# A transformer block on one core: a new written-out order for about nine hundred operations

## The chip, the core and the metric

The kernel runs on one core of a Trainium2 chip. The metric is the device time of one execution in microseconds (us). Five instruction streams run side by side, each in its own order: TensorE (PE in the profile: matrix products; PEld are its weight loads), VectorE (DVE), ScalarE (ACT), GpSimd (POOL), and SyncE (SP), which here only issues DMAs: loads, stores and transposing copies. An instruction that waits for another engine holds up everything behind it in its own stream.

## The reference

The input x has 2048 rows (one batch) of D = 640, bf16. There are H = 32 heads of 20 and F = 1536.

```python
def _A_ref(x, wqkv, w_phi, wo):
    ... # q, k, v = heads of x @ wqkv
    pq = jnp.einsum("bhsd,hdf->bhsf", q, w_phi)
    pk = jnp.einsum("bhsd,hdf->bhsf", k, w_phi)
    phi_q = jnp.concatenate([_softmax(pq, axis=-1), _softmax(-pq, axis=-1)], axis=-1)
    phi_k = jnp.concatenate([_softmax(pk, axis=-1), _softmax(-pk, axis=-1)], axis=-1)
    kv = jnp.einsum("bhsf,bhsd->bhfd", phi_k, v)
    z  = jnp.einsum("bhsf->bhf", phi_k)
    num = jnp.einsum("bhqf,bhfd->bhqd", phi_q, kv)
    den = jnp.einsum("bhqf,bhf->bhq", phi_q, z)[..., None] + 1e-6
    o = num / den
    return (...) @ wo          # heads put side by side again
def _B_ref(x, w_gate, w_up, w_down):
    return ((x @ w_gate) * (x @ w_up)) @ w_down     # written as einsums
x = A_x
h = x + _A_ref(_layernorm(x, axis=-1), A_wqkv, A_w_phi, A_wo)
h2 = h + _B_ref(_layernorm(h, axis=-1), B_w_gate, B_w_up, B_w_down)
return h2
```

The attention is linear: the sum over all rows (`kv`, `z`) must be complete before the first row of `num` can be formed. The block ends with a gated product without a nonlinearity.

## The kernel before

**Tiles.** The rows are cut into 16 tiles of 128. An operation's name carries its tile: Qb5 is operation Qb of tile 5. Line numbers are those of the kernel before; the changed file's are 21 lower from `class Buf` on, since its table of the order has 21 lines fewer.

**Preparation.** `w_phi` is folded into the K and Q parts of `wqkv` on TensorE. Loads of x and weights (L285) are x0, x1, x2, x3, x4, x6, x8, x10, x12, x14 (the later ones two tiles each), wk, wv, w5, wg, wu, wd, wo. Ph0 to Ph2 (L380, POOL or DVE) lay out `w_phi`; WT0 to WT4 (L392) transpose the K weights on TensorE and WTe copies them out; F1_0 to F1_4 (L411) are the five K folds, F0_0 to F0_4 the five Q folds, and Fe copies each out of PSUM. The Q weights are transposed by SP's DMAs wqt0 to wqt4 (L309). Before that, small products warm0 to warm21 (L367, L372) run on zeros.

**Attention, per tile t.** L1s, L1a (L428, L431, DVE), L1l, L1e (L436, L439, ACT) and L1n (L443, one element per row, POOL or DVE) give the statistics of the first normalisation; xn (L453 on DVE, L451 on ACT) applies it; xt transposes the result, on TensorE for tiles 0 and 1 (L462, copied out by xte, L251), by an SP DMA for the others (L471). V, K and Q (L482) are projections of ten matmuls of 320 columns each (for tiles 0 and 1 cut into five pairs, K0_0 to K0_4). Ve copies V out of PSUM (L251, `evac`, ACT or DVE). Of K, Kx (L494, ACT, two instructions) takes exp of plus and minus the value, Ks (L498, DVE) sums over each head, Kr and Ke (L501, L503, ACT) form the reciprocal through ln and exp, Kn (L518, POOL) multiplies, and KV (L526, eleven small matmuls) adds to `kv` and `z`, which stay in two PSUM banks until KVe (L533, DVE) takes them out. Of Q, Qx (L551 and a small L553, ACT, twice) takes the exps, Qs (L556, DVE) sums, Qr (L559, ACT) takes the ln, Qb (L563, POOL or DVE, 32 elements per row) subtracts, Qe (L566, ACT) takes an exp, Qn (L570, POOL) scales one half, and qT (L575) is an SP transposing DMA. N (L588) is the product with `kv`; dd, rl, rd (L602, L606 to L612, DVE or ACT) prepare the division and o (L615, DVE) does it; oT (L619) is an SP transposing DMA; O (L625) the product with `wo`.

**Second part, per tile and block.** h (L631, DVE) adds the residual and sums the row; hc (L639 on DVE, L640 on ACT) centres; hT (L653) is an SP transposing DMA; L2q (L642, ACT), L2v (L646, POOL or DVE, one element per row) and L2r (L649, DVE) give the row's scale, which is applied only at the end. The gate and up products U (L668) run over blocks of tiles: block 0 is tiles 0 and 1, block 1 tiles 2 to 5, block 2 tiles 6 to 9, block 3 tiles 10 to 13, block 4 tiles 14 and 15, each in 12 pieces of F, gate and up apart (U1_3_0 is block 1, piece 3, gate). g (L673, ACT) copies the gate product out, u (L676, DVE) multiplies. D (L687) is the down product of a tile, y (L699, DVE) scales and adds, w (L701) stores. Tile 15's down product is cut into three pieces.

**What sets the order.** Nothing is scheduled on the chip. A table, PLAN, holds for each operation a number, which engine of its alternatives it uses, and which buffers of a pool it takes:

```python
    _f = _t.split(":")
    PLAN[_f[0]] = (float(_f[1]), int(_f[2] or 0) if len(_f) > 2 else 0,
                   tuple(int(_v) for _v in _f[3].split(",")) if len(_f) > 3 else ())
```

`Graph.op` reads the entry; `alts` lists the engine of the code first and the other one second, so `Qb5:369:1` means rank 369, second engine (for Qb: POOL first, DVE second; for Ve: ACT first, DVE second). `arrange` sorts all operations by the number and appends each to its engine's stream:

```python
    for o in sorted(G.ops, key=lambda o: (o.key, o.i)):
        o.start = o.key
        order[o.eng].append(o)
```

It also adds the waits that follow from a buffer taken a second time. `emit` turns all dependences into waits on the engines' counters, leaving out those that another wait already covers. The numbers in the table are used for sorting alone. The table of before holds times in us, that of the changed kernel ranks from 0 to 1029.

Of the kernel before, what the change touches and what calls it, by code (L numbers as in the profile page):

```python
# [53 lines left out]
x1:0.78:1 ekz:0.78 x0:0.78 zero:0.91 id0:1.014 warm0:1.127 id1:1.252 x3:1.26:1 wk3:1.26:1 warm1:1.345 va1:1.496 warm2:1.564 w5:1.74:1 warm3:1.782 warm4:2.001  # L54
warm5:2.219 wk0:2.22:1 eps:2.326 gl0:2.357 warm6:2.437 gla:2.518 warm7:2.656 wk4:2.7:1 glb:2.822 warm8:2.874::0 warm9:3.093 wk1:3.18 warm10:3.311 warm11:3.529
wk2:3.66:1 L1s1:3.725 warm12:3.748 warm13:3.966 x4:4.14 warm14:4.185 warm15:4.403 L1s0:4.512 wv1:4.62 warm16:4.621 warm17:4.84 wv0:5.1:1 L1a1:5.299 L1s3:5.408
WT3:5.446::1 L1l1:5.532 wv2:5.58:1 Ph2:5.775 L1e1:5.858 warm18:5.902 warm19:6.011 wv3:6.06 WTe3:6.1:1 warm20:6.12 L1a0:6.195 xn1:6.304::0 Ph1:6.369 x2:6.54
# [4 lines left out]
wqt1:12.163 L1s2:12.225 L1e4:12.321 V0_0:12.369::6 K1_4:12.64 V1_1:12.911 L1n5:13.012:1 Kx1_0:13.11::0 V0_1:13.182 xn5:13.296::3 V0_2:13.453 Kx1_1:13.694
V0_3:13.724 L1a2:13.826 xt5:13.934 L1s7:13.935 V0_4:13.995 K0_2:14.266 L1l2:14.278 K0_3:14.537 L1e2:14.604 Ve0:14.697::0 Ks1:14.722::0 V1_2:14.808 L1n2:14.884
V1_3:15.079 Sz:15.108 wqt0:15.244 xn2:15.281:1:0 L1n4:15.287 V1_4:15.35 K3:15.621::4 L1s6:16.115 Kr1:16.234 Ke1:16.525 xt2:16.554 x12:16.671:1 Kn1:16.859
K0_4:16.977 L1a6:17.025 xn4:17.134::1 Kx3_0:17.177::1 V3:17.248::6 L1s8:17.664 Kx3_1:17.761 wqt2:17.864 Ve1:18.345::1 L1a7:18.451 L1s9:18.56 K5:18.604::4
L1l6:18.929 xt4:19.174 L1e6:19.255 Ks3:19.347::1 Ve3:19.348::2 L1n7:19.535 L1n6:19.759 Kx0_0:19.932::2 V5:19.96::0 rqz:19.983 wqt3:20.484 Kx0_1:20.516
xn7:20.74::2 Kx5_0:21.1::3 xn6:21.27::3 K2:21.316::6 Kx5_1:21.684 L1a8:21.8 xt6:21.908 L1a9:21.909 Ks0:22.018::2 Kr3:22.268 Ke3:22.559 V2:22.672::2
Ve5:22.705::3 Kn3:22.893 xt7:23.218 Kx2_0:23.289::4 Ks5:23.411::3 Kx2_1:23.873 V4:24.028::4 Ve2:24.457::4 x10:24.528 L1s12:24.804 x14:25.008 L1l8:25.041
L1e8:25.367 F0_0:25.384::0 Kr0:25.46 wg2:25.488 Ks2:25.591::0 L1n8:25.647 F0_2:25.703::6 Ke0:25.751 L1n9:25.871 Ve4:25.897::5 wg0:25.968 V6:26.022::2 Kn0:26.095
Fe0_0:26.481 L1s13:26.984 xn9:27.065:1:0 F0_4:27.378::4 K4:27.697::0 Kr5:27.88 Fe0_4:27.895:1 xt9:28.018 Ve6:28.026::6 mk0:28.408 mk1:28.572 Kr2:28.61  # L70
L1s11:28.635 Ke2:28.901 Fe0_2:29.047 KV0:29.053::4,5 Kn2:29.235 wd1:29.328 KV1:29.386 L1s10:29.422 Kx4_0:29.631::2 K7:29.719::2 L1s14:30.209 Kx4_1:30.215
F0_3:31.075::6 L1a14:31.119 L1a10:31.228 Kx7_0:31.275::0 xn8:31.337::1 V7:31.394::0 smz:31.548 Fe0_3:31.859 L1a11:31.867 xt8:31.975 Ks4:31.976::1 Kx7_1:32.443
KV2:32.75 Ke5:33.027 KV3:33.083 L1l10:33.173 wg1:33.285 L1s15:33.369 F0_1:33.416::6 L1e10:33.499 K6:33.735::2 L1n11:33.779 Fe0_1:33.933 Kn5:34.003
L1n10:34.156:1 L1a13:34.331 xn11:34.44::3 Kr4:34.517 Ve7:34.663::7 L1a15:34.97 xt11:35.078 L1a12:35.079 K9:35.091::6 Ks7:35.188::2 Ke4:35.247 Kx6_0:35.393::4
Kx6_1:35.977 Kn4:36.316 wd0:36.388 Q0_0:36.447::0 L1l12:36.561 Ks6:36.713::0 Q0_1:36.719 Kx9_0:36.743::1 Q0_2:36.991 Q0_3:37.263 Kr7:37.327 Q0_4:37.535
Ke7:37.618 L1e12:37.764 Q1_0:37.807::2 Kx9_1:37.857 Q1_1:38.079 xn10:38.106::2 Q1_2:38.351 Kr6:38.441 Q1_3:38.623 mk2:38.629 L1n12:38.636:1 Ke6:38.732
Ks9:38.811::3 Q1_4:38.895 L1n15:38.9 Kn6:39.123 KV4:39.167 Qx1_0:39.365::0 K8:39.5::6 Qx1_1:39.975 L1n13:40.204:1 xn13:40.488::0 Qx0_0:40.585::1 KV5:40.856
# [851 lines left out]
```

## Time and profile before

| | |
|---|---|
| median of 3 runs | 271.48 us (271.42, 271.48, 271.83) |
| span of the profiled execution | 270.1 us |
| PE, PEld busy | 264.2, 177.9 us |
| DVE, ACT, POOL busy | 160.0, 124.0, 71.3 us |
| HBM read, written | 11.00, 2.62 MB |

For the profiled execution only its span is given, not a time of its own; the span goes from the first instruction to the last. A row of a timeline gives start and length in us (of the stretch from first start to last end, where it groups several, as `x3` tells), engine, line, operation, output and inputs with their sizes; in brackets idle time of the engine before it and what ended that. In the slices the span is cut into 40 equal parts (6.75 us each), each digit being the busy tenths of one. A PE row's length is that of its pipelined instructions, so it is longer than the distance to the next row.

### The profile page before, as it was taken

The numbers are of one execution on the slowest core, as the hardware profiler recorded it, in microseconds if no ns is written. First come the engines' busy times: TensorE is split into PE (matmuls) and PEld (weight loads), VectorE is DVE, ScalarE is ACT, GpSimd is POOL, SyncE is SP. The second block draws the span as 40 slices with busy tenths as digits, with TensorE's granted clock in tenths as the row PEclk, the third lists the DMA queues.
The fourth block names the chain that finished last, engine by engine and source line by source line (L and its number), as shares of the span: only waits on it lengthen the run. The fifth ranks groups of instructions, "written<-read, shape, count | busy, mean of one in ns | idle before, by whom it ended". The sixth has DMA issues, their size and how long they took to land.

```text
span 270.1 us, 5186 instructions
## 1 busy us (share of the span) xinstructions
PE 264.2 (98%) x2092; PEld 177.9 (66%) x2105; DVE 160.0 (59%) x294; ACT 124.0 (46%) x316; POOL 71.3 (26%) x89
## 2 busy tenths in 40 slices
...
DVE  4999799978988998577664253332342311423432
...
GB/s 200 318 168 136 249 222 129 302 183 245 204 106 143 163 126 149 140 123 64 171 93 2 0 0 36 57 106 1 73 12 2 0 0 51 49 1 0 27 49 61
DMA packets 71752, 28.09 MB, mean 104 GB/s; under 512 B 59056, under 2 KB 71728, under 8 KB 71728
## 3 DMA queue, kind: packets, MB, share of 16 engines
...
q8 instruction: 16, 0.26, 0.4%
q14 instruction: 8, 0.07, 0.1%
HBM read 11.00 MB, written 2.62 MB: 50 GB/s over the span
## 4 chain that ended last, share of the span: by engine, by line
PE 90%; DMA 5%; DVE 2%; ACT 1%; issue 1%; SPq 1%; DVEq 0%
PE ps L668 36%; PE ps L482 24%; PE ps L687 19%; PE ps L625 6%; DMA scratch<-ph 2%; PE ps L526 2%; PE ps L588 2%; DMA Wp<-o 2%; DMA x_all<-in_A_x_dram 1%; PE ps L411 1%; SPq L653 1%; DVE st L428 0%; ACT Wp L251 0%; DVE st L429 0%; DVE ev L676 0%
## 5 line engine op out<-in xcount | busy, mean ns | idle before, releaser
L668 PE MATMUL ps<-xnT,Wgu 128*128 128x512 bf16 (+1 forms) x587 | 106.0, 335 | 0.7
L668 PEld LDWEIGHTS ps<-xnT,Wgu 128*128 128x128 bf16 x600 | 58.3, 98 | 43.4
L673 ACT ACTIVATE gt<-ps 128x512 bf16<-128x512 f32 (+1 forms) x60 | 29.7, 509 | 100.9 <-PE ps L668 62.9
L482 PE MATMUL ps<-Wp,xnT 128*128 128x320 bf16 (+1 forms) x480 | 68.6, 298 | 0.0
L482 PEld LDWEIGHTS ps<-Wp,xnT 128*128 128x128 bf16 x480 | 45.5, 97 | 17.2 <-issue 0.2
L676 DVE TENSOR_TENSOR ev<-ps,gt 128x512 bf16<-128x512 f32 (+1 forms) x60 | 33.6, 579 | 36.5 <-PE ps L668 27.8
L687 PE MATMUL ps<-Wd,ev 128*128 128x320 bf16 (+2 forms) x396 | 53.9, 295 | 0.0
L687 PEld LDWEIGHTS ps<-Wd,ev 128*128 128x128 bf16 x396 | 38.1, 98 | 15.3 <-DVE ev L676 0.2
L699 DVE SCALAR_TENSOR_TENSOR Wp<-ps,rs,x_all 128x640 bf16<-128x640 f32 (+3 forms) x18 | 14.6, 810 | 49.3 <-PE ps L687 49.1
L518 POOL TENSOR_TENSOR ek<-ek,SR 128x1280 bf16<-128x1280 bf16 x16 | 37.5, 2358 | 5.2 <-ACT SR L503 5.1
L551 ACT ACTIVATE ph<-ps 128x600 bf16<-128x600 f32 x32 | 21.4, 680 | 8.0 <-PE ps L482 6.9
L556 DVE TENSOR_REDUCE S<-ph 128x66 f32<-128x1320 bf16 x16 | 23.9, 1516 | 1.8 <-ACT ph L553 1.8
L625 PE MATMUL ps<-Wo,Wp 128*128 128x320 bf16 x160 | 23.9, 299 | 0.2
L498 DVE TENSOR_REDUCE SR<-ek 128x64 f32<-128x1280 bf16 x16 | 23.3, 1468 | 1.0 <-ACT ek L494 1.0
L570 POOL TENSOR_TENSOR ph<-ph,RQ 128x660 bf16<-128x660 bf16 x16 | 20.7, 1308 | 8.9 <-ACT RQ L566 8.9
L646 POOL TENSOR_SCALAR ln<-mv 128x1 f32<-128x1 f32 x12 | 2.3, 191 | 75.7 <-ACT ek L642 75.1
L494 ACT ACTIVATE ek<-ps 128x640 bf16<-128x640 f32 x32 | 21.2, 719 | 2.2 <-PE ps L482 1.5
L625 PEld LDWEIGHTS ps<-Wo,Wp 128*128 128x128 bf16 x160 | 15.3, 98 | 6.4 <-DMA Wp<-o 0.4
L631 DVE SCALAR_TENSOR_TENSOR x_all<-ps,x_all 128x640 bf16<-128x640 f32 x16 | 13.1, 821 | 6.4 <-PE ps L625 6.4
L615 DVE TENSOR_TENSOR o<-ps,sm 128x660 bf16<-128x660 f32 x16 | 13.4, 840 | 0.9 <-ACT sm L608 0.6
L642 ACT ACTIVATE ek<-x_all,mv 128x640 bf16<-128x640 bf16 x16 | 13.1, 821 | 0.0
L251 ACT ACTIVATE ev<-ps 128x640 bf16<-128x640 f32 x16 | 11.2, 704 | 1.1 <-PE ps L482 1.1
...
## 6 DMA issues: line engine op xcount, KB each, us to landing
out_dram<-Wp SPq DMA_DIRECT2D x15, 160.0 KB, 1.8
...
Wp<-in_A_wqkv_dram SPq DMA_DIRECT2D x5, 160.0 KB, 4.7
ev<-in_A_wqkv_dram SPq DMA_DIRECT2D x4, 160.0 KB, 4.2
x_all<-in_A_x_dram SPq DMA_DIRECT2D x3, 160.0 KB, 3.2
```

The costliest lines, as they stand in the source:

```text
L482: ins = e.matmul(pb(b, hb)[:, 0:n1 - n0], lhsT=T["xnT"][:, NC - 1 - c, P * t:P * (t + 1)], rhs=T["Wp"][:, POS[kind], c, n0:n1], start=(c = ...
L494: G.op("act", "%sx%d_%d" % (nm, t, s), lambda e, s=s, b=b, ek=ek: e.activation(out=T["ek"][:, ek.slots[0], 0:2 * D].rearrange("p (b h s f) ...
L498: G.op("dve", "%ss%d" % (nm, t), lambda e, ek=ek, sr=sr: e.tensor_reduce(out=T["SR"][:, sr.slots[0], 0, :], in_=T["ek"][:, ek.slots[0], 0: ...
L518: G.op("pool", "Kn%d" % t, lambda e, eng, ek=ek, sr=sr: e.tensor_tensor(out=T["ek"][:, ek.slots[0], 0:2 * D].rearrange("p (h f) -> p h f", ...
L551: e.activation(out=v[:, 0:10].rearrange("p (b g) j f -> p b g j f", b=2), in_=pp(b, 0, 300).rearrange("p b (g j f) -> p b g j f", j=3, f=D ...
L556: G.op("dve", "Qs%d" % t, lambda e, t=t, ph=ph: e.tensor_reduce(out=T["S"][:, t, 0:66].rearrange("p (g k) -> p g k", k=6), in_=pv(ph).rear ...
L570: return e.tensor_tensor(out=v, in0=v, in1=T["RQ"][:, rq.slots[0], 1, 0:33].rearrange("p (g j) -> p g j", j=3).unsqueeze(3).to_broadcast([ ...
L625: ins = e.matmul(pb(b, hb)[:, 0:320], lhsT=T["oT"][:, oT.slots[0], c, :], rhs=T["Wo"][:, c, 320 * hb:320 * (hb + 1)], start=(c == 0), stop ...
L668: ins = e.matmul(pb(b)[:, 0:n], lhsT=T["Wgu"][:, gu, c, P * ft:P * (ft + 1)], rhs=T["xnT"][:, NC - 1 - c, o0:o0 + n], start=(c == 0), stop ...
L673: G.op("act", "g%d_%d" % (bi, ft), lambda e, pg=pg, gt=gt, n=n: e.activation(out=T["gt"][:, gt.slots[0], 0:n], in_=pb(pg)[:, 0:n], func=AF ...
L676: o_ = G.op("dve", "u%d_%d" % (bi, ft), lambda e, pu=pu, gt=gt, hh=hh, ft=ft, n=n: e.tensor_tensor(out=T["hh"][:, hh.slots[0], ft, 0:n], i ...
L687: ins = e.matmul(pb(b, hb)[:, 0:w], lhsT=T["hh"][:, hh.slots[0], ft, P * tt:P * (tt + 1)], rhs=T["Wd"][:, ft, c0 + w * hb:c0 + w * (hb + 1 ...
```

## The change

Only the table PLAN is replaced. Every operation is still there with the same shapes; changed are the places in the five streams, some engines, and the buffers that follow from the new order. The first seventeen loads keep their queue and their order within it.

Engines that change: from ACT to DVE Ve8, Ve9, Ve11, Ve14, xn2, xn9, Fe0_1, WTe1, hc5, hc9, hc10; from DVE to ACT xn10, WTe0, Fe0_4, hc3, hc6, hc7, hc11 to hc15; from POOL to DVE Ph0, L1n2, L1n3, L1n9, Qb3, Qb5, Qb12, Qb14, Qb15, L2v0, L2v5, L2v12, L2v15; from DVE to POOL L1n5, L1n10, L1n12, L1n13, Qb4, L2v7. The loads x8, x10, x14 and wg1 move from SP's queue to ACT's, x12 from ACT's to SP's.

TensorE's stream at the front, before: WT0 xt1 WT4 WT1 warm21 F1_0 F1_3 WT2 xt0 F1_1 F1_4 F1_2 K0_0 and so on; after: WT0 xt1 WT4 xt0 F1_3 WT1 WT2 F1_4 F1_0 F1_1 F1_2 V0_0 and so on. In the stretch that follows K of tile 11, the streams are:

```
PE before    K11 KV6 Q3 KV7 Q9 K10 K15 V8 V9 V13 V11 Q2 KV8 K13 Q4 KV9 K12 V10
PE after     K11 Q9 KV7 K10 K15 V13 Q2 V10 V8 K13 KV8 V9 Q4 KV9 KV10 K12 K14
DVE before   Ks11 Qs3 Qs9 Qs5 Ks10 L1n14 xn14 Ks15 Qb9 Qs2 Ks13 Qb2 Ks12 Qs4 Ks14 Qb4
DVE after    Ks11 Ks10 Qs3 Qb5 Ks15 Ve8 Qb3 Qs2 Ve9 Qb2 Qs9 Ks13 Ks12 Ks14 Qb9 Qs10 Ve11
POOL before  Kn8 Qn1 Qb0 Qb3 Kn11 Qn3 Qn0 Qb5 Kn10 Qn9 Kn15 Kn13 Qn5 Qn2 Kn12 Kn14 Qn4
POOL after   Kn8 Qn1 mk2 Qn0 Kn11 Qn5 Kn10 Qn3 Kn15 Qn2 Kn13 smz Kn12 Kn14 Qn9 Qb4
ACT after    Kx11 (2) Qx3_1 Qr0 Kr8 Ke8 Qe1 Qx9 (2) Kx10 (2) Kx15_0 Qe0 Qr5 Ve13 Kr11 Ke11 Kx15_1
```

Of the first seventeen loads fifteen stand on SP's queue and two (x1, wk3) on ACT's. SP's queue behind its fifteen and xt3, the first transpose, before: x8, wqt4, wqt1, xt5, wqt0, xt2, wqt2, xt4, wqt3, xt6, xt7, x10, x14, wg2, wg0, xt9; after: wqt2, wqt3, xt2, wqt1, xt5, xt4, wqt4, wqt0, xt6, xt7, x12, wd0, wo2, wu0, xt9. N of tile 15 moves behind more products of blocks 0 and 1. TensorE's last products are D14 D11 D13 D12 D10 D15_1 D15_2 before and D14 D13 D15_0 D12 D11 D10 D15_1 D15_2 after.

The diff replaces 98 lines of the table by 77; cut to the stretches named:

```diff
 PLAN = {}
 for _t in """
...
-WT0:6.546::2 L1l0:6.685 Ph0:6.761 L1a3:6.834 xt1:6.971::3 wv4:7.02:1 WTe0:7.023:1 L1l3:7.067 L1e0:7.249 WT4:7.25::4 L1e3:7.393 xte1:7.486 xn0:7.487::1 x6:7.5
-L1n3:7.673 WT1:7.746::5 phz:7.897 WTe4:8.017:1 warm21:8.025 F1_0:8.134::6 WTe1:8.223:1 xn3:8.425::2 F1_3:8.453::0 WT2:8.772::2 Fe1_0:8.808:1 xt0:9.051::3
-xt3:9.063 WTe2:9.249:1 F1_1:9.33::4 Fe1_3:9.392 F1_4:9.649::6 xte0:9.657:1 Fe1_1:9.976 L1s4:10.065 F1_2:10.153::0 x8:10.373 K0_0:10.472::2 Fe1_2:10.67:1
...
+WTe3:57:1 xn1:58::1 x2:59 WT0:60::0 xn0:61::0 Ph2:62 xt1:63::1 wv4:64:1 WTe0:65 Ph0:66:1 WT4:67::2 L1a3:68 phz:69 x6:70 xt0:71::3 xte1:72 WTe4:73:1 F1_3:74::6
+WT1:75::4 xte0:76:1 L1l3:77 WT2:78::5 Fe1_3:79 WTe1:80 F1_4:81::0 F1_0:82::2 WTe2:83:1 L1e3:84 Fe1_4:85:1 F1_1:86::6 L1n3:87:1 xn3:88::2 F1_2:89::4 Fe1_0:90:1
+V0_0:91::0 L1s5:92 xt3:93 V0_1:94 Fe1_1:95 V0_2:96 V1_0:97::2 Fe1_2:98:1 V0_3:99 L1s2:100 K0_0:101::6 wqt2:102 K0_1:103 K1_0:104::4 V0_4:105 L1a2:106 L1s4:107
...
+K0_4:125 Kx1_0:126::0 xt2:127 L1n5:128 V1_1:129 L1n4:130 V1_2:131 Kx1_1:132 L1s6:133 V1_3:134 V1_4:135 Kx0_0:136::1 wqt1:137 K3:138::0 xn5:139::1 x8:140:1
+L1a7:141 L1a6:142 xn4:143::0 Kx0_1:144 xt5:145 Ks1:146::1 V3:147::4 x14:148:1 Ve1:149::1 xt4:150 L1l6:151 Ks0:152::0 K2:153::6 x10:154:1 Kx3_0:155::3 wqt4:156
...
-Qs1:41.018 xt13:41.126 Q5:41.189::2 Qx0_1:41.195 Kn7:41.437 Kx8_0:41.805::2 Kx8_1:42.389 xt10:42.436 xn15:42.453::1 K11:42.556::0 Kr9:42.973 Qx5_0:43.119::2
-Ks8:43.125::1 Qr1:43.729::0 xt15:43.746 Ke9:43.875 KV6:43.912 Qx5_1:44.021 Qb1:44.073 Q3:44.245::6 Kn9:44.272 Qs0:44.518 Kx11_0:44.631::3 wu2:45.056
-Kx11_1:45.215 wu3:45.536 KV7:45.612 Kr8:45.799 Q9:45.945::2 xn12:45.953::3 wu0:46.016 Ke8:46.09 Qx3_0:46.236::3 Ks11:46.483::0 wu1:46.496 Kn8:46.585
-Qx3_1:46.846 K10:47.312::0 Qe1:47.456 Qx9_0:47.575::4 Qs3:47.876 Qx9_1:48.185 K15:48.668::6 Kr11:48.795 Qn1:48.898 Kx10_0:48.941::4 Qs9:49.311 Qr0:49.525::1
-Qr3:49.671::2 Kx10_1:49.817 V8:50.024::2 Qb0:50.163 qT1:50.233::0 Qb3:50.362 Ke11:50.401 Kn11:50.735 Qs5:50.746 V9:51.38::0 Ve8:51.58::0 xt12:51.723
-Kx15_0:52.164::0 Ks10:52.181::2 V13:52.736::2 Kx15_1:52.748 wo2:53.033 Qe3:53.332 Qe0:53.451 Ve9:53.57::1 L1n14:53.574:1 Qn3:53.639 xn14:53.858::0 V11:54.092::6
-Ve13:54.292::4 Ks15:54.388::3 xt14:54.536 Qr9:54.876::3 Qn0:54.904 Qr5:55.022::0 Kr10:55.168 Q2:55.448::0 Ve11:55.648::2 Qb9:55.781:1 qT3:55.846::1 Qb5:56.169
-Ke10:56.232 Kn10:56.566 KV8:56.815 Qx2_0:57.013::5 K13:57.148::2 qT0:57.336::2 Qx2_1:57.623 Kr15:58.233 Qe9:58.379 Qs2:58.418 Q4:58.504::6 Kx13_0:58.704::2
-Qn9:58.879 Kx13_1:59.288 wd2:59.516 KV9:59.871 Ke15:59.872 wo0:59.996 Ks13:60.024::1 Qx4_0:60.069::0 K12:60.204::0 Kn15:60.206 qT9:60.476::3 Qx4_1:60.679
...
+KV6:316 Qx5_1:317 L1n14:318:1 K11:319::0 Qs0:320 xt13:321 Qx3_0:322::3 Qb1:323 Ke9:324 Q9:325::6 wg3:326 Kn9:327 Ks8:328::3 Kx11_0:329::4 xt12:330 Kx11_1:331
+KV7:332 Qx3_1:333 xn14:334::3 K10:335::0 wu1:336 Qr0:337::1 Qs5:338 Kr8:339 Qb0:340 Ke8:341 wu3:342 Qe1:343 Qx9_0:344::5 Kn8:345 K15:346::2 Qx9_1:347
+Ks11:348::2 Kx10_0:349::1 V13:350::6 Kx10_1:351 Qn1:352 Kx15_0:353::2 Ks10:354::0 Qe0:355 Q2:356::0 Qr5:357::2 Ve13:358::1 mk2:359 Qn0:360 Kr11:361 Qs3:362
+Ke11:363 Kx15_1:364 V10:365::6 Qx2_0:366::4 Kn11:367 qT0:368::0 Qb5:369:1 Ks15:370::3 Qe5:371 Kr10:372 V8:373::2 Ve10:374::6 Ke10:375 xt14:376 Qr3:377::0
+Qx2_1:378 K13:379::6 Ve8:380:1:4 Qn5:381 qT1:382::5 Qb3:383:1 Qs2:384 KV8:385 Kn10:386 V9:387::0 Kx13_0:388::0 wu2:389 Kr15:390 Qr2:391::3 Ke15:392 Kx13_1:393
+Q4:394::2 Ve9:395:1:4 Qe3:396 Qn3:397 Qb2:398:1 Qs9:399 KV9:400 Qx4_0:401::1 KV10:402 K12:403::0 Kn15:404 qT3:405::1 Qe2:406 Qx4_1:407 Ks13:408::2 K14:409::6
...
-o14:110.404::2 U1_0_0:110.936::7 L2q3:111.099 u0_7:111.159 hT9:111.572 g0_8:111.939::2 N15:112.015::4 g1_0:112.213::0 U0_10_1:112.348::6 dd15:112.546::1
...
+U1_9_0:703::4 h13:704 o6:705::2 hc13:706::3 U1_6_0:707::6 oT6:708::0 N15:709::0 U1_3_0:710::7 dd15:711::2 L2v1:712:1 oT14:713::2 U1_8_0:714::2 g1_3:715::3
...
 """.split():
```

More of the change, by code (lines that the diff above doesn't have):

```diff
@@ L53 @@
 for _t in """
[L54 to L57, printed above, removed]
@@ L62 @@
[L62 to L65, printed above, removed]
```

130 lines of the change are left out of this document (59 added, 71 removed).

## The prediction, made before the changed kernel was run

> **What bounds the kernel now.** I read the page first (parts 1 and 2), then ten-microsecond windows, the chain of waits, and the timelines of single engines.
>
> ```profile
> span 270.1 us, 5186 instructions
> PE 264.2 (98%) x2092; PEld 177.9 (66%) x2105; DVE 160.0 (59%) x294; ACT 124.0 (46%) x316; POOL 71.3 (26%) x89
> DVE  4999799978988998577664253332342311423432
> ```
> ```profile
> 50.00:60.00 10.00, 10.00 (x84) 7.26 (x83) 8.05 (x9) 9.05 (x25) 9.57 (x9) 1.00 1.16 240
> 60.00:70.00 10.00, 10.00 (x92) 7.33 (x91) 9.03 (x8) 9.23 (x30) 9.96 (x7) 1.00 1.22 258
> 80.00:90.00 10.00, 9.76 (x97) 6.91 (x96) 8.95 (x17) 4.89 (x17) 4.35 (x5) 1.00 0.85 150
> 110.00:120.00 10.00, 9.46 (x73) 5.99 (x74) 6.56 (x13) 6.51 (x18) 0.25 (x2) 1.00 1.01 140
> ```
> ```profile
> 46.29 10.89 PE ps L482 x80
> 57.18 0.33 PE ps L526 x11
> 84.39 4.20 DMA Wp<-o
> 88.63 1.53 PE ps L625 x10
> 107.51 5.44 DMA scratch<-ph
> 113.00 0.51 PE ps L588 x11
> ```
>
> TensorE has work at all times but a few. A window row gives busy microseconds of PE, PEld, DVE, ACT, POOL, then granted clock (1.00), DMA share and GB/s. PE lacks 0.24 at 80 to 90, where a PE group began only when a transpose of `o` had landed (88.63), and 0.54 at 110 to 120, behind a transpose of `ph` (113.00). The eighty matmuls in 10.89 give 0.136 each, 1.36 per ten; this is the yardstick for PE below. The edit keeps every instruction, so it can only remove idle time of PE or add it.
>
> At one place I weigh a rule. The Trainium skill, Perfetto Trace Analysis, section Identifying the Most-Contended Engine, says that busy matmul time is no measure of distance to the limit and that weight-load time is; by it, 66% would leave a third of the span, some 90 us, to be won. The row of 46.29 decides against it here: order alone does not shorten 0.136 us per matmul.
>
> **The change, part by part.**
>
> *Gain at the front.* In the old order the last of the five K folds waits:
>
> ```profile
> 10.19 0.32 PEld L411 LDWEIGHTS ps<-Phi,scratch 128*128 128x128 bf16 x6 [0.35 <-DVE xnT L251]
> ```
> That is for the copy of a transposed tile. The new order does both TensorE transposes before any fold, so this copy is done long before; what follows (V of tile 0) finds its weights loaded. Gain 0.35; bounds 0 and 0.35.
>
> *Gain in the middle.* The two holes above, 0.78 in all. A record of PE outlasts its slot:
>
> ```profile
> L482 PE MATMUL ps<-Wp,xnT 128*128 128x320 bf16 (+1 forms) x480 | 68.6, 298 | 0.0
> ```
> The mean is 298 ns against 136, so each hole is understated by 0.16; with three (88.6 is two, before and behind tile 9's output product), 0.78 + 3 x 0.16 = 1.26. The new order moves the late tiles' N and O behind more gate and up products: the product that stood at 113.00 (N of tile 15) now comes some 10 us later by PE work, its transpose as well, with other work between. I take this gain whole at 113 and leave 0.2 of the hole at 80 to 90, because DVE's work there stays as dense. Bounds of what is left: 0 and 0.5 (twice the 0.24 seen).
>
> *Cost at the SP queue.* Its first transpose waits for the normalised tile 3, which comes behind four copies instead of two:
>
> ```profile
> 9.15 0.49 DVE L251 COPY scratch<-ps 128x640 bf16<-128x640 bf16 x1
> ```
> ```profile
> 9.14 1.31 SPq L471 DMA_TRANSPOSE xnT<-xn  x1
> 10.50 0.57 SPq L285 DMA_DIRECT2D x_all<-in_A_x_dram  x1
> 22.49 2.60 SPq L471 DMA_TRANSPOSE xnT<-xn  x2
> ```
> ACT's queue:
> ```profile
> 16.48 0.44 ACTq L285 DMA_DIRECT2D x_all<-in_A_x_dram  x1
> ```
> Eleven transposes of 1.31 follow one another in both orders, but x8, which stood among them, now goes through ACT's queue, as do x10 and x14. Two more copies of 0.49, and the small work between, delay the start by 1.0 to 1.3, and the load that left gives back 0.57. Tile 6's transpose then issues 0.4 to 0.7 later than at 22.49, while V of tile 6 comes a little earlier on PE. The worst case is that this 0.7 has no cover at all, the best that all of it has: bounds 0 and 0.7. I take 0.2, since one chunk of fold work stands before V of tile 6 in both orders. The loads behind it (wd0, wo2, wu0 early; wg1 on ACT, late) are needed only after 90 us: nothing, unless they delay tile 9's transpose, within the same bound. ACT issues three loads by 22 us in place of one: 2 x 0.44 = 0.9 more there, beside its copies, of which the normalised tiles 2 and 9 leave for DVE: I take nothing; at worst 0.9, beside that 0.7 and not on top, as both delay the same stretch of PE.
>
> *Cost on DVE, 50 to 62 us: the term that decides.* Four copies of V (Ve8, Ve9, Ve11, Ve14, L251) move from ACT to DVE, and so do Qb5 and Qb3 (L563) from POOL, while Qb4 goes back; Qb2 and Qb9 stay on DVE. Of the first normalisations two come to DVE and one leaves it, before 40 us; of the second (L639 on DVE, L640 on ACT) eight go to ACT and three come back, most of them after 115 us, where the slices show DVE at six tenths or less; the one-element L443 and L646 swap places: nothing, and at worst one copy's 0.5.
>
> ```profile
> L563 DVE TENSOR_TENSOR RQ<-RQ 128x32 f32<-128x32 f32 x3 | 3.3, 1097 | 0.2 <-ACT RQ L559 0.2
> L251 DVE CAST Wp<-ps 128x640 bf16<-128x640 f32 x1 | 0.8, 823 | 0.5 <-PE ps L411 0.5
> L358 POOL TENSOR_SCALAR_AFFINE_SELECT mask<-mask 128x33 bf16<-128x33 bf16 x2 | 0.6, 312 | 0.1
> ```
> DVE:
> ```profile
> 47.33 1.48 DVE L498 TENSOR_REDUCE SR<-ek 128x64 f32<-128x1280 bf16 x1
> 48.73 4.39 DVE L556 TENSOR_REDUCE S<-ph 128x66 f32<-128x1320 bf16 x3
> 56.65 0.18 DVE L563 TENSOR_TENSOR RQ<-RQ 128x32 f32<-128x32 f32 x1
> 61.94 0.90 DVE L563 TENSOR_TENSOR RQ<-RQ 128x32 f32<-128x32 f32 x1 [0.20 <-ACT RQ L559]
> 67.79 2.21 DVE L563 TENSOR_TENSOR RQ<-RQ 128x32 f32<-128x32 f32 x1
> ```
> POOL:
> ```profile
> 56.50 0.24 POOL L563 TENSOR_TENSOR RQ<-RQ 128x32 f32<-128x32 f32 x1
> 56.78 2.36 POOL L518 TENSOR_TENSOR ek<-ek,SR 128x1280 bf16<-128x1280 bf16 x1
> 60.44 4.67 POOL L518 TENSOR_TENSOR ek<-ek,SR 128x1280 bf16<-128x1280 bf16 x2
> 65.06 2.57 POOL L570 TENSOR_TENSOR ph<-ph,RQ 128x660 bf16<-128x660 bf16 x2
> 67.59 4.68 POOL L518 TENSOR_TENSOR ek<-ek,SR 128x1280 bf16<-128x1280 bf16 x2
> ```
> The same 32-element subtraction takes 0.18, 0.90 or 2.21 on DVE. The 0.18 ran between two POOL instructions. The 2.21 began at 67.79, 0.20 after POOL had begun a 2.36 long L518, and ended at 70.00 with it; the 0.90 ended at 62.84, at the border of the pair that began at 60.44. So it waits until POOL is through with what it has begun. In the old order these waits, 0.72 + 2.03, fell where PE's next needs were far off. The Trainium skill, SBUF — State Buffer, section Who interferes with whom, says the same: a DVE instruction with two SBUF inputs and a GpSimd one that reads SBUF share a port, whoever is first blocks the other for its whole length. The trace agrees (2.21 against 2.36), and it is the rule that speaks against this change.
>
> Now Qb5's place. ACT's rows, for the run-up:
> ```profile
> 45.24 1.42 ACT L494 ACTIVATE ek<-ps 128x640 bf16<-128x640 f32 x2
> 46.40 0.39 ACT L501 ACTIVATE SR<-SR 128x64 f32<-128x64 f32 x1
> 46.83 0.26 ACT L503 ACTIVATE SR<-SR 128x64 f32<-128x64 f32 x1
> 46.99 0.65 ACT L551 ACTIVATE ph<-ps 128x600 bf16<-128x600 f32 x1
> 47.62 0.67 ACT L551 ACTIVATE ph<-ps 128x600 bf16<-128x600 f32 x1
> 48.26 0.25 ACT L566 ACTIVATE RQ<-RQ 128x32 f32<-128x32 f32 x1
> 48.38 0.69 ACT L551 ACTIVATE ph<-ps 128x600 bf16<-128x600 f32 x1
> ```
> Time 0 is the end of K of tile 11 on PE. New ACT order: Kx11 twice (46.40 - 45.24 = 1.16), half of Qx3 (47.62 - 46.99 = 0.63), then Qr0, Kr8, Ke8 at 0.26 each: done at 2.6, and POOL starts Kn8. POOL then runs Kn8 2.34, Qn1 1.28, mk2 0.31, Qn0 1.28 (halves of 4.67 and 2.57) and starts Kn11 at 7.8. ACT goes on with Qe1 0.12 (48.26 to 48.38; it starts 0.1 before Ke8's record ends, as 46.99 in 46.83 + 0.26), Qx9 2 x 0.63, Kx10 0.58 + 0.71 (half of 1.16, and the rest of 1.42 - 0.71): 5.2; then DVE does Ks10 1.40 (47.33 to 48.73), Qs3 1.45 (a third of 4.39) and comes to Qb5 at 8.05. That is 0.2 after Kn11 began, as at 67.79. Qb5 ends with Kn11, at 7.8 + 2.36 + 0.05 = 10.2. Behind it on DVE: Ks15 1.40, Ve8 0.82, done 12.45. PE, eight groups of 1.36 and one KV of 0.33 later, wants Ve8 for KV8 at 11.2: PE waits 1.25. Without the block Ve8, behind V of tile 8 at 9.85, would be ready at 10.7.
>
> Qb3 comes at 12.45. POOL, having waited for Qb5 to give Qe5 (0.25), runs Qn5 from 10.5 to 11.8 and Kn10 to 14.15; Qb3 ends 14.2, Qs2 1.45, Ve9 0.82: 16.5. KV9 is due at 12.45 + 0.33 + 2 x 1.36 = 15.5: PE waits 1.0 more. Qb2 then finds POOL waiting for Qe3, and behind Qb9 stands one reduction before the copy of V of tile 11, for which PE has to get there first: nothing. Sum 2.25; bounds 0 (Qb5 before Kn11) and 3.2 (another block of 0.9, as at 61.94, at Qb9). A check without chains: DVE's idle time at 50 to 70 is 1.95 + 0.97, the old blocks give back 2.75, in all 5.7; the new work is 4 x 0.82 for the copies and 2.15 + 1.75 for the blocks, 7.2: it does not fit, by 1.5.
>
> *The rest of the order.* From 130 us on (slice 20) the slices show DVE at seven tenths or less, the transposes come well before their products, and the last pieces (tile 10, two pieces of tile 15, their adds and stores) end in the same order: nothing; 0.3 either way.
>
> *Sum.* -0.35 - 1.26 + 0.2 + 0.2 + 2.25 = +1.05. The profiled span is 270.1; the median, 271.48, lies 1.4 above it with start and end, which do not change. 271.48 + 1.05 = 272.5.
>
> **Rivals.**
> A, faster: Qb5 reaches DVE before Kn11 begins. It needs 0.2 us, a tenth of one reduction; then it waits at most for Qn0, Ve8 and Ve9 are in time, and the gains stand: 271.48 - 1.61 + 0.4 = 270.3. For it: the margin is small against sums of seven rows. Against it: both sides start from Ke8, and if DVE is later, Qb5 falls deeper into Kn11's 2.36.
> B, about as before: one of the two blocks is missed or covered (Kn10 a little later, or ACT late): 270.3 + 1.0 to 1.25, so 271.3 to 271.5.
> C, no change of use: the holes at 88 and 113 stay, being SP's, and no block costs PE anything: 271.5 - 0.35 + 0.2 = 271.3. Against it: 10 us of other PE work now stands before N of tile 15.
> D, slower still: the third block, and the SP queue's bound of 0.7: 273.6.
>
> **How the numbers follow.** Forecast 0.52 (272.5; alone 271.9 to 273.1), A 0.28, B and C 0.13, D 0.07. About 0.2%, 0.54 us, is what can be told from no change here: 270.94 to 272.02. Faster 0.30 (A and the edge of B), same 0.13, slower 0.57. The range 270.0 to 273.4 holds A, B and the forecast.
>
> **What would show it.** Right: L563 on DVE with single times near 2.2 and 1.8 between 50 and 62 us, a PE wait for DVE L251 before L526 twice there, no PE hole near 113, the first projection 0.3 earlier. Wrong: L563 on DVE near 0.2, or blocked with PE unbroken (then ACT's or PE's rows were mispriced); a PE wait for the transposes at 25 us of over 0.7.

## The result: 2.3% slower, six times the forecast

The changed kernel takes 277.82 us (median, 277.55 to 278.24); the kernel before, on the same chip, 271.65. The ratio is 1.0229, 95% interval 1.0213 to 1.0246. The forecast was 272.5, range 270.0 to 273.4: the sign was right, the size was not. The times here and below are medians without the executions that took over 1.5% longer than the fastest of the same kernel (two of qb_pool, one of w_late_xn3). The page of the changed kernel has these lines:

```profile
span 276.5 us, 5189 instructions
PE 265.5 (96%) x2091; PEld 178.3 (64%) x2105; DVE 162.1 (59%) x301; ACT 122.7 (44%) x316; POOL 69.4 (25%) x82
PE   6968999989999999999999999999999999999996
PEclk9997999999999999999999999999999999999999
```

TensorE's work is the same; it is idle longer, in one place above all (the third slice, 13.8 to 20.7 us), and in the next slice its granted clock is down to seven tenths. Windows of 2 us (busy PE, PEld, DVE, ACT, POOL, then clock, DMA share, GB/s) show both (clocks of 0.55 and 0.59 are means over a window; the last section has the stretch itself):

```profile
18.00:20.00 2.00, 0.49 (x4) 0.12 (x2) 2.00 (x4) 0.85 (x2) 0.50 (x2) 1.00 0.89 204
20.00:22.00 2.00, 0.10 (x1) 0.11 (x2) 1.74 (x5) 0.00 (x0) 0.00 (x0) 1.00 1.14 202
22.00:24.00 2.00, 2.00 (x9) 1.12 (x9) 0.00 (x0) 0.00 (x0) 0.00 (x0) 0.55 1.31 170
24.00:26.00 2.00, 2.00 (x10) 1.22 (x9) 0.72 (x2) 0.99 (x3) 0.56 (x1) 0.59 1.02 198
26.00:28.00 2.00, 2.00 (x17) 1.44 (x15) 0.17 (x1) 1.50 (x3) 1.94 (x2) 1.00 0.77 147
```

The chain of waits names the cause: start, length, what.

```profile
14.84 7.02 DMA xnT<-xn
21.85 0.05 issue
21.90 8.23 PE ps L461 x47
```

K of tile 2 could have begun on TensorE at 18.3 and began at 21.90, when the transpose xt2, which delivers its input, had landed. That transpose was issued at 14.84 and was 7.02 us under way. ACT issued three loads of x around it (queue rows, changed kernel):

```profile
14.73 0.39 ACTq L264 DMA_DIRECT2D x_all<-in_A_x_dram  x1
15.19 0.46 ACTq L264 DMA_DIRECT2D x_all<-in_A_x_dram  x1
16.36 0.39 ACTq L264 DMA_DIRECT2D x_all<-in_A_x_dram  x1
```

The list of DMA issues between 14 and 20 us gives the median time to landing in its last column; first the changed kernel, then the kernel before:

```profile
x_all<-in_A_x_dram ACTq DMA_DIRECT2D x3, 320.0 KB, 6.3
xnT<-xn SPq DMA_TRANSPOSE x3, 6.9
```
```profile
x_all<-in_A_x_dram ACTq DMA_DIRECT2D x1, 320.0 KB, 3.9
xnT<-xn SPq DMA_TRANSPOSE x3, 2.8
```

The other term came as forecast, almost to the tenth. Rows of POOL, DVE, ACT and PE of the changed kernel, in this order:

```profile
58.60 2.36 POOL L497 TENSOR_TENSOR ek<-ek,SR 128x1280 bf16<-128x1280 bf16 x1
62.61 2.36 POOL L497 TENSOR_TENSOR ek<-ek,SR 128x1280 bf16<-128x1280 bf16 x1
```
```profile
58.90 2.11 DVE L542 TENSOR_TENSOR RQ<-RQ 128x32 f32<-128x32 f32 x1
62.33 0.81 DVE L230 CAST ev<-ps 128x640 bf16<-128x640 f32 x1
63.06 1.96 DVE L542 TENSOR_TENSOR RQ<-RQ 128x32 f32<-128x32 f32 x1
66.38 0.81 DVE L230 CAST ev<-ps 128x640 bf16<-128x640 f32 x1
```
```profile
61.04 0.23 ACT L545 ACTIVATE RQ<-RQ 128x32 f32<-128x32 f32 x1 [1.89 <-DVE RQ L542]
61.32 0.69 ACT L230 ACTIVATE ev<-ps 128x640 bf16<-128x640 f32 x1
```
```profile
62.06 1.53 PE L461 MATMUL ps<-Wp,xnT 128*128 128x320 bf16 x10 [1.36 <-ACT ev L230]
67.25 0.85 PE L505 MATMUL ps<-ev,ek 128*128 128x63 bf16 x22 [0.58 <-DVE ev L230]
86.08 0.85 PE L567 MATMUL ps<-KVm,scratch 128*128 128x63 bf16 x22 [0.28 <-DMA scratch<-ph]
```

Qb5 reached DVE 0.30 after Kn11 had begun and took 2.11; Qb3 0.45 after Kn10, 1.96. TensorE lost 1.52 before K of tile 13 (62.06), 0.75 before KV of tile 9 (67.25), and 0.44 before N of tile 9 (86.08). These figures are the distance between the starts of two successive matmuls, less what the first of them usually takes (0.136 for 320 columns). The ledger by this measure: 3.57 of waiting for xt2; 1.01 and 0.67 that K and V of tile 2 then took longer at the lower clock; 2.27 behind the blocks; 0.44; less 0.36 won at the front and the 1.16 of the three old holes (0.30, 0.26 and 0.60). That is +6.4, and TensorE's last product starts 6.4 later (273.4 against 267.0).

### The profile page after: what moved, and what is told of

It reads as the page before. It is cut to its first block, busy times and chain, and to the rows that moved or that the text cites. A ratio compares the mean times of both kernels' runs of the same rounds, so it can differ in the third digit from the quotient of the medians.

```text
span 276.5 us, 5189 instructions
## 1 busy us (share of the span) xinstructions
PE 265.5 (96%) x2091; PEld 178.3 (64%) x2105; DVE 162.1 (59%) x301; ACT 122.7 (44%) x316; POOL 69.4 (25%) x82
## 4 chain that ended last, share of the span: by engine, by line
PE 78%; DMA 6%; DVE 5%; POOL 5%; ACT 2%; SPq 2%; issue 1%; DVEq 0%
PE ps L647 37%; PE ps L666 19%; PE ps L461 11%; PE ps L604 8%; POOL ek L497 3%; DMA xnT<-xn 3%; SPq L264 2%; DMA scratch<-ph 2%; DMA x_all<-in_A_x_dram 2%; PE ps L567 2%; DVE RQ L542 1%; POOL ph L549 1%; ACT ek L473 1%; DVE S L535 1%; PE ps L505 1%
## 5 line engine op out<-in xcount | busy, mean ns | idle before, releaser
L461 PE MATMUL ps<-Wp,xnT 128*128 128x320 bf16 (+1 forms) x480 | 70.1, 303 | 4.8 <-DMA xnT<-xn 3.4
L461 PEld LDWEIGHTS ps<-Wp,xnT 128*128 128x128 bf16 x480 | 46.2, 99 | 23.6 <-DMA xnT<-xn 3.7
L497 POOL TENSOR_TENSOR ek<-ek,SR 128x1280 bf16<-128x1280 bf16 x16 | 37.6, 2357 | 10.0 <-ACT SR L482 9.9
L625 POOL TENSOR_SCALAR ln<-mv 128x1 f32<-128x1 f32 x9 | 1.7, 192 | 58.7 <-ACT ek L621 58.2
L432 DVE TENSOR_SCALAR xn<-x_all,mv,rs 128x640 bf16<-128x640 bf16 x15 | 8.8, 593 | 3.3 <-DMA xnT<-xn 2.8
```

The lines of the kernel that those rows point to most:

```text
L461: ins = e.matmul(pb(b, hb)[:, 0:n1 - n0], lhsT=T["xnT"][:, NC - 1 - c, P * t:P * (t + 1)], rhs=T["Wp"][:, POS[kind], c, n0:n1], start=(c = ...
L497: G.op("pool", "Kn%d" % t, lambda e, eng, ek=ek, sr=sr: e.tensor_tensor(out=T["ek"][:, ek.slots[0], 0:2 * D].rearrange("p (h f) -> p h f", ...
```

## The experiments

All kernels below are edits of the table PLAN (fill also adds an operation); "x8:93.5" puts x8 at rank 93.5 on its first engine (SP), a third field 1 on the second (ACT). Each ratio is of means, to the kernel before on the same chip. "A wait of n" is what TensorE lost, by the measure of the ledger; the expectations quote some of these waits up to 0.15 longer, with part of a matmul's own time in them. A profile shows one execution, in some runs 1 to 2 us off the median; where that bears on a reading, its time is given.

**loads_sp: the three loads back on SP.**

```diff
-x8:140:1 x14:148:1 x10:154:1
+x8:93.5 x10:183.3 x14:183.6
```

> The changed kernel with x8, x10 and x14 back on SP's queue (x8 right behind the first transpose, x10 and x14 behind the transpose of tile 7). Theory L: the wait of 3.71 us for xT of tile 2 and the slow clock behind it come from the three loads that ACT issues at 14.7 to 16.8 us, which share the DMA engines with SP's transposes. Then tile 2's transpose lands at about 18.5 instead of 21.85, K of tile 2 waits under 0.5, and 277.8 - 5.3 + 0.3 gives 272.5 to 273. Rival O: the wait comes from the order alone (K of tile 2 moved ahead of K of tile 5 on PE, two weight transposes ahead of it on SP, a start 1.25 us later). Then the wait stays over 3 us and the time is 277 to 278.

Measured 277.95, ratio 1.0219 (1.0195 to 1.0244). The time says theory O, the profile does not (PE and DVE of loads_sp):

```profile
13.70 11.57 PE L461 MATMUL ps<-Wp,xnT 128*128 128x320 bf16 x84
26.70 1.53 PE L461 MATMUL ps<-Wp,xnT 128*128 128x320 bf16 x10 [0.82 <-DMA xnT<-xn]
32.72 4.24 PE L461 MATMUL ps<-Wp,xnT 128*128 128x320 bf16 x30 [1.49 <-ACT SR L482]
```
```profile
29.13 0.49 DVE L407 BATCH_NORM_STATS2 st<-x_all 128x6 f32<-128x320 bf16 x1 [5.08 <-DMA x_all<-in_A_x_dram]
```

From 13.70 to 25.27 TensorE runs without a gap: xt2 landed at 17.96, and the hole and the slow clock are gone. The loss came back elsewhere: 1.3 at 25 us (transposes late), and 3.0 behind DVE, which stood 5.08 us at the statistics of tile 11, because x10 now landed at 29.1. The new order of DVE was made for an early x10. Moving one load moved the wait.

**two_loads_late: x10 and x14 later on ACT.**

```diff
-x14:148:1 x10:154:1
+x10:184.3:1 x14:184.6:1
```

> The changed kernel with x10 and x14 still on ACT's queue, but issued some 8 us later, behind L1e8; x8 stays at 14.7. Theory L: only 320 of the 960 KB lie over tile 2's transpose; it lands at 19.0 to 20.0, K of tile 2 waits 1 to 2 us, 274 to 275.5. Rival O: no change, 277.8.

Measured 276.0, ratio 1.0142 (1.0120 to 1.0163). xt2 landed at 19.69 and K of tile 2 waited 1.15, as theory L said: the wait follows the bytes (0, 320 and 960 KB issued around it on ACT's queue give 0, 1.15 and 3.57; two later runs with 0 KB, loads_sp_dve and loads_sp_dve_qb, have 0.40 and 0.50). The time is above the expectation; DVE again waited for x10 (3.15, to 28.6 us), and TensorE lost 0.46, 0.50 and 0.92 between 27 and 40 us.

**before_loads_act: the same fault put into the kernel before.**

```diff
-x10:24.528 x14:25.008
+x14:15.27:1 x10:16.68:1
```

> The kernel before with x10 and x14 on ACT's queue beside x12, issued at about 15.3 and 16.9 us instead of 25 on SP's. Theory L: tile 2's transpose lands at 23.5 to 25 instead of 21.14, PE waits 2 to 3.5 us before K of tile 2 (due at 21.28) or already before K of tile 5, the clock falls behind it: 274 to 277. Rival O: nothing, 271.4 to 271.9.

Measured 273.7, ratio 1.0066 (1.0030 to 1.0102). xt5 landed at 19.39 and xt2 at 23.38 instead of 17.26 and 21.14; PE waited 0.95 before K of tile 5 and 1.26 before K of tile 2. The mechanism is there without the rest of the new order; the time lies just under the expected range.

**qb_pool: the two subtractions back on POOL.**

```diff
-Qb5:369:1 Qb3:383:1
+Qb5:366.5 Qb3:385.5
```

> The changed kernel with Qb5 and Qb3 on POOL again, Qb5 ahead of Kn11 and Qb3 ahead of Kn10. Theory B: the waits of PE of 1.67 at 62 us (for Ve10, which stands on ACT behind Qe5, which waits for the blocked Qb5) and 0.90 at 67 us (for Ve9) come from the two blocked subtractions; without them both are gone: 277.8 - 2.57 gives 275.2. Rival V: the four copies of V are too much for DVE by themselves; then Ve9 stays late, a wait of 1 us or more stays, 276.3 to 277.

Measured 273.7, ratio 1.0066 (1.0036 to 1.0096). The span of the profiled execution (275.25) is 273.5 against 276.5, and PE of qb_pool shows no gap from 52 to 91 us; two of its rows:

```profile
52.20 9.68 PE L461 MATMUL ps<-Wp,xnT 128*128 128x320 bf16 x70
85.21 2.88 PE L604 MATMUL ps<-Wo,Wp 128*128 128x320 bf16 x20
```

All of 2.27 + 0.44 is gone with the copies of V still on DVE: the blocks were the cause, not DVE's load. The other 0.3 of the difference in span was not traced. The median lies below the expected 275.2: four of these eight executions, with a mean granted clock of 1.000, took 272.2 to 273.0, the four others, with 0.994 as in all four of the changed kernel, 274.4 to 275.3.

**fill: PE kept busy during the wait.**

```diff
+def fl(e, b=b):
+    for _ in range(30):
+        ins = e.matmul(pb(b, 0)[:, 0:256], lhsT=T["zero"][:, 0:P], rhs=T["zero"][:, :], start=True, stop=True)
+    return ins
+G.op("pe", "fillK2", fl, 3.3, LT, [z_b], [b], key)
-K2:153::6
+fillK2:152.5::6 K2:153
```

> The changed kernel with thirty matmuls of 256 columns on a tile of zeros put on PE ahead of K of tile 2, into the bank that K of tile 2 overwrites: 3.3 us of work in the place of the idle time of 3.7, nothing else. Theory C: the 1.6 us that V of tile 2 and K of tile 5 lose behind the wait (2.1 to 2.2 each instead of 1.34, granted clock 0.55 to 0.59) come from PE's idleness; with PE at work the clock stays at 1.00 and 277.8 - 1.6 gives 276.2. Rival: those two wait for something else (a transpose, a bank); then nothing changes, 277.8.

Measured 277.27, ratio 1.0221 (1.0191 to 1.0252), span 275.1. Windows of fill:

```profile
22.00:24.00 2.00, 2.00 (x17) 1.43 (x16) 0.72 (x2) 0.94 (x3) 0.01 (x1) 1.00 1.12 221
24.00:26.00 2.00, 2.00 (x17) 1.43 (x16) 0.25 (x1) 1.63 (x4) 2.00 (x1) 1.00 0.88 148
```

The clock stays at 1.00 and 17 matmuls fit where 9 or 10 did; K of tile 5 began 2.07 earlier: 0.39 because K of tile 2 began earlier (xt2 landed at 20.76 in this execution, and the filling matmuls ran to 21.50), 1.68 by the clock. So the slow clock came from the idleness. (It was K and V of tile 2 that it slowed, not V of tile 2 and K of tile 5, as I wrote.) Of the gain 1.25 was lost again before O of tile 1 at 89.9, whose transpose of `o` now came last; the time missed the expected 276.2, and its ratio is not clear of the changed kernel's 1.0229.

**loads_sp_dve and loads_sp_dve_qb: DVE's order put right for a late x10, then also the blocks removed.**

```diff
-L1s11:189 L1s10:200 L1a11:206 L1a10:209
+L1s11:215.3 L1s10:215.5 L1a11:215.6 L1a10:215.7
```

> Run loads_sp with DVE's statistics of tiles 10 and 11 (four instructions that read x10) moved behind the sum of tile 5's K. In loads_sp DVE stood idle for 5.08 us at 24 us until x10 had landed, and PE lost 1.71 and 1.37 behind it (before K of tile 7 and Q of tile 1). Theory L: the hole at 18 us was the loads', and what took its place is DVE's order, made for an early x10; with both put right 277.95 - 3.1 gives 274.9, with 1.4 left at 25 us (the last two weight transposes and tile 6's, late on SP). Rival O: the order is at fault elsewhere as well and other waits follow: 276 or more.

> The same with Qb5 and Qb3 on POOL. Waits of 2.57 us and, as in qb_pool, that of 0.48 before N of tile 9 go: 274.9 - 3.0 gives 271.9, the time of the kernel before, with the 1.4 us at 25 us left.

Measured 276.11, ratio 1.0179 (1.0140 to 1.0219), and 273.08, ratio 1.0073 (1.0044 to 1.0103). Both are 1.2 over the expectation. In both profiles the waits before K of tile 7 and Q of tile 1 went, and one of 2.64 (1.34 in the second) came before K of tile 9, for xt9. The profiled executions took 277.32 and 274.99, more than the medians, so how much of the 1.2 this wait is remains open. xt9 stands on SP's queue behind x10, x14, x12 and the weights wd0, wo2 and wu0.

**x8_act_early, w_late, w_late_xn3: fewer bytes ahead of xt9.**

```diff
-x8:93.5
+x8:107.5:1                              (x8_act_early, on top of loads_sp_dve_qb)
-wd0:196 wo2:199 wu0:202
+wd0:286 wo2:286.3 wu0:286.6             (w_late)
-L1e3:84 L1n3:87:1 xn3:88::2
+L1e3:78.5 L1n3:82.3:1 xn3:82.6::2       (w_late_xn3)
```

> The same with x8 on ACT's queue again, but issued at about 11.8 us, behind the last copy of a K fold, instead of 11.7 us on SP's. SP's transposes come 0.57 earlier, x8 shares the engines with tile 3's transpose only, as in the kernel before: the wait at 25 us falls by 0.5 to 0.6, 271.3. If x8 holds up a transpose as x8 at 14.7 did in two_loads_late, K of tile 3 or of tile 2 waits 0.5 or more: 272 or above.

> Run x8_act_early with the loads of wd0, wo2 and wu0 (480 KB each) moved on SP's queue from ahead of tile 9's transpose to behind tile 10's. In x8_act_early that transpose landed at 37.88 us and PE lost 2.04 before K of tile 9. Theory D: a transpose lands when the bytes issued ahead of it have passed, here three x loads and three weight loads; without the weight loads it lands by 34 and the wait goes: 273.67 - 2.04 gives 271.6. Rival: the transpose is late because its tile is normalised late on DVE; then the wait stays, 273.7.

> The same with the normalisation of tile 3 ahead of one copy on DVE (WTe2) and its scale (L1e3) ahead of one on ACT, so that SP's first transpose starts at about 9.6 us instead of 10.1 to 10.4. Theory D: the waits of 0.20 and 1.16 at 25 us (for the last weight transpose and tile 6's) fall by the 0.6 to 0.8 that the start comes earlier, at the price of 0.3 to 0.5 at the last K fold: 271.6 - 0.3 gives 271.3 (270.6 to 271.8). If these two waits are not the queue's start, nothing is gained and 271.9 is left.

Measured 273.67, ratio 1.0109 (1.0060 to 1.0159); 277.44, ratio 1.0197 (1.0162 to 1.0232); 274.65, ratio 1.0123 (1.0095 to 1.0152). PE of x8_act_early, then PE and SP's queue of w_late:

```profile
37.92 2.63 PE L461 MATMUL ps<-Wp,xnT 128*128 128x320 bf16 x18 [1.93 <-DMA xnT<-xn]
```
```profile
52.20 1.53 PE L461 MATMUL ps<-Wp,xnT 128*128 128x320 bf16 x10 [2.49 <-DMA xnT<-xn]
54.74 5.48 PE L461 MATMUL ps<-Wp,xnT 128*128 128x320 bf16 x39 [1.01 <-DMA xnT<-xn]
```
```profile
44.28 3.87 SPq L450 DMA_TRANSPOSE xnT<-xn  x1
```

x8 on ACT gained nothing at 25 us (a wait of 1.19 against one of 1.21). In w_late xt9 landed at 32.18 and its wait went, as theory D said; but the weights now stood ahead of xt15 and xt13, which landed at 52.15 and 54.69, and TensorE lost 2.65 and 1.17 there. The profiled execution took 275.22; the other three took 277.1 to 277.8. The row of 44.28 shows the queue itself held up: a transpose whose like took 1.4 in the median of this run took 3.87 to issue behind five weight loads. With the early start of SP's transposes (w_late_xn3) there is no wait before V of tile 6, at a cost of 0.68 at the K folds; but the profile of w_late has only 0.10 before V of tile 6 as well.

**w_last, w_last_xn3: the weights behind the last transposes of `xn`.**

```diff
-wd0:286 wo2:286.3 wu0:286.6 wg0:296 wd2:311
+wd0:376.6 wo2:376.3 wu0:376.9 wg0:371 wd2:372
```

> Run w_late with five weight loads (wd0, wo2, wu0, wg0, wd2) moved once more, behind tile 12's transpose, so that no weight load but wg2 and wd1 stands ahead of the last four transposes of normalised tiles. Theory D: the waits of 2.69 and 1.20 before K of tile 15 and V of tile 13 (transposes landing at 52.15 and 54.69, behind five weight loads in one queue) go and no other transposing DMA becomes late, since the transposes of the features are needed from 78 us on only: 277.44 - 3.9 gives 273.5 against the median, 275.22 - 3.9 gives 271.3 against the profiled execution. Rival: PE then waits for DVE or ACT in the same stretch instead, since the order leaves them no slack: over 274.

> The same with tile 3's normalisation early, as in w_late_xn3. Theory D: 275.04 - 3.6 gives 271.4, the time of the kernel before; with both blocks and all late transposes gone the new order's gains (0.36 at the front, 1.4 in the middle) may show, 270.5 at best. Rival: as above, over 273.

Measured 276.7, ratio 1.0172 (1.0138 to 1.0205), and 275.98, ratio 1.0144 (1.0108 to 1.0180). PE, a window and SP's queue of w_last:

```profile
71.67 5.60 PE L461 MATMUL ps<-Wp,xnT 128*128 128x320 bf16 x30 [2.92 <-ACT ph L532]
```
```profile
72.00:74.00 2.00, 2.00 (x9) 1.12 (x8) 1.18 (x1) 1.86 (x6) 2.00 (x1) 0.50 1.19 331
```
```profile
61.06 4.69 SPq L554 DMA_TRANSPOSE scratch<-ph  x1
```

The waits before K of tile 15 and V of tile 13 went, and I was wrong that a feature transpose is not needed before 78 us: qT1 (61.06, landed at 70.03) frees the buffer into which Q of tile 10 is exponentiated. ACT stood for it, and TensorE lost 3.08, and 1.4 to the clock, at 70 us.

**spread: the weights issued where SP is idle.**

```diff
-wg2:236 wg0:371 wd1:280 wd0:376.6
+wg2:231 wg0:232 wd1:233 wd0:234
-wu0:376.9 xt14:376 wo2:376.3 wd2:372
+wu0:343 xt14:334.5 wo2:383.5 wd2:419
```

> Run w_last_xn3 with the weight loads spread out so that SP issues them in its idle stretches: wg2, wg0, wd1, wd0 behind tile 8's transpose, wg3, wu1, wu3, wu0 behind tile 13's with the transposes of tiles 12 and 14 ahead of most, the others singly between the feature transposes. Theory D: in w_last PE waited 3.24 and 1.3 (with the slow clock) at 70 us for the exps of Q of tile 10, whose buffer came free with the feature transpose of tile 1, landed at 70.03 behind five loads. With no more than four loads ahead of any transpose and PE's need late, these go: 275.98 - 4.7 gives 271.3. Rival (DVE and ACT have no slack in this order): over 273.5, with PE waiting for DVE or ACT where no DMA is late behind them.

Measured 271.64, ratio 0.9991 (0.9977 to 1.0005): the time of the kernel before, as theory D said. Its span, and two rows of PE of spread, which cover the places of the holes before K of tile 2, before K of tile 15 and V of tile 13 (w_late), and before K of tile 13 (the blocks):

```profile
span 269.9 us, 5203 instructions
```
```profile
10.69 15.10 PE L461 MATMUL ps<-Wp,xnT 128*128 128x320 bf16 x110
48.60 9.68 PE L461 MATMUL ps<-Wp,xnT 128*128 128x320 bf16 x70
```

It still has the changed kernel's order of PE and, but for the moves named, of DVE, ACT and POOL.

**What is left to win: before_n15, spread_dve, spread_dve_no_xn3.**

```diff
-N15:112.015::4 dd15:112.546::1 rl15:112.762
+N15:112.95::4 dd15:113.0::1 rl15:113.05           (before_n15, in the kernel before)
-L1l10:233 L1s13:226 L1s12:229
+L1l10:234.5 L1s13:237.3 L1s12:237.6               (spread_dve, on top of spread)
```

> The kernel before with one product moved: N of tile 15 behind two more up products (U0_10_1, U0_8_1), and the division that reads it behind h10 on DVE. It tests a term of the gain by itself. If that wait of PE (0.54 by the window, 0.81 by the distance of the rows) is worth what was taken for it, the time falls by 0.5 to 0.8, 270.8 to 271.1. If the wait is only passed on to the next product (O of tile 13 or 15), 271.6.

> Run spread with DVE's statistics of tiles 12 and 13 behind the sum of tile 4's K and one small ACT instruction (L1l10) behind Kx4_1. In spread PE still lost 0.28 before K of tile 6, 0.66 before Q of tile 1 and 0.15 before KV of tile 4, all behind these. If a wait removed here is worth its length, 271.64 - 1.0 gives 270.6, 0.4% below the kernel before. If it is passed on, as the wait removed in before_n15 was, 271.4 to 271.8.

> The same without the early normalisation of tile 3. The two waits of 0.65 at the K folds (9.6 and 10.4 us) go, SP's first transpose starts 0.4 to 0.7 later. Theory D: the transposes of tiles 3 and 6 then come 0.2 to 0.7 late for PE (as in w_last and w_late); the two about cancel, 270.4 to 271.0.

Measured 271.66, ratio 1.0007 (0.9989 to 1.0025); 271.55, ratio 0.9988 (0.9973 to 1.0002); 272.57, ratio 1.0012 (0.9990 to 1.0034). None beats the kernel before beyond its interval. PE of before_n15:

```profile
114.81 0.50 PE L588 MATMUL ps<-KVm,scratch 128*128 128x63 bf16 x11
118.83 2.33 PE L668 MATMUL ps<-xnT,Wgu 128*128 128x512 bf16 x10 [0.23 <-DVE ev L676]
```

The wait of 0.60 before N of tile 15 is gone, and 0.40 appeared at 118.83, behind DVE, which now comes later to the division of tile 15 and to what follows it. Two thirds were passed on; the rest is less than the interval, and the profiled execution took 272.93, 1.3 above the median. In spread_dve the wait before Q of tile 1 stayed (0.62 at 37.6 became 0.60 at 37.5, now for a copy of a Q fold) and one of 0.39 came, for the exps of Q of tile 1 (42.1). spread_dve_no_xn3, expected at 270.4 to 271.0, has the late transposes back, with waits of 0.78 and 0.96 at 27 to 28.5 us in the profiled execution (274.18).

## Why the prediction was wrong

**The step that failed: "Cost at the SP queue", taken as 0.2 within "bounds 0 and 0.7".** It measured 5.2 by the ledger (3.57 of waiting and 1.68 of slow clock). loads_sp took this away in the profile, but its time did not fall, so no time confirms the figure alone. The step counted when SP issues, and for the first transpose it was right: it started 1.25 later (10.39 against 9.14; I had 1.0 to 1.3). Tile 6's was issued 2.35 later, though (24.84 against 22.49; I had 0.4 to 0.7; in loads_sp, without the three loads on ACT, 0.64). And the step took landing for issuing plus a constant. The sentence "x8 ... now goes through ACT's queue, as do x10 and x14" was booked as a relief of 0.57 for SP; on the DMA engines these loads put 960 KB beside four transposes, and the landing of a transpose grew from 2.8 to 6.9. The trace of before could have shown it: the load x12, the quoted row of 16.48, had the transpose of tile 2 beside it (issued at 17.22) land 3.9 after issue, where that of tile 5, issued at 14.59, took 2.7. The cost was bounded by rows of issue alone. I also looked at tile 6's transpose and not at tile 2's, though the new order brings K of tile 2 ahead of K of tile 5, from 21.3 to 18.3.

The Trainium skill, DMA: Bandwidth & Descriptors, section Issuing engines are not separate DMA queues, says that DMAs started by different engines run on the same sixteen DMA engines and interleave, and that a second issuing engine saves only the issue time. The runs agree (0, 1.15 and 3.57 for 0, 320 and 960 KB on ACT's queue), and this rule should have been a rival.

**Also in that step:** "nothing, unless they delay tile 9's transpose, within the same bound". The three early weight loads cost nothing in the changed kernel, probably because TensorE came there 5 us later; without the first hole, the wait for xt9 was 1.3 to 2.6 (loads_sp_dve, loads_sp_dve_qb, x8_act_early), and w_late removed it by moving them.

**A second effect had no place in the sum:** the clock after a long wait, 1.7 of the 5.2 (fill). It contradicts the sentence that the edit "can only remove idle time of PE or add it": K and V of tile 2 ran with no idle time between their matmuls and still took 1.68 more.

**Cost on DVE: right.** Forecast 2.15 and 1.75 for Qb5 and Qb3, measured 2.11 and 1.96; forecast 2.25 on TensorE, measured 2.27; qb_pool removed it all. Its two parts were forecast as 1.25 and 1.0 and came as 1.52 and 0.75, so that the sum fits to 0.02 is luck. The path of the first was another one. I had a late Ve8 holding KV8; but Qe5 on ACT also waits for Qb5, and behind it Ve10, whose PSUM bank K of tile 13 needs (the 1.89 of idle at 61.04). I had named who waits behind Qb5 on DVE and on POOL, not on ACT. Rival A, in which Qb5 slips ahead, missed by 0.30.

**Gain at the front: right** (0.36 against 0.35). **Gain in the middle:** the three old holes went (1.16 against 1.26), but 0.44 came back before N of tile 9, more than the 0.2 left for it. Whether such a gain is worth its length is doubtful: before_n15 removed the largest part, and no gain could be measured.

**The other rivals.** B and C had no part for the loads, and D 0.7 for the whole queue, so none could hold the result. D's 273.6 is also 0.3 below what its own terms add up to (272.5 + 0.9 for the third block + 0.5 for the queue).

What stays open is whether this order can be faster than the old one: spread and spread_dve are 0.1% below it with intervals that reach 1.0002 to 1.0005. How much of xt2's delay is the shared engines and how much the order inside each of them was not measured apart. Nor is it shown which single part of spread is needed, as it differs from the changed kernel in the loads, the two blocks and the early statistics together.
